# Re-planning a two-layer linear-attention kernel: DMA transposes given queue time, small matmuls cut into pieces between large ones, masks built first

## The chip, the cores and the metric

The kernel runs on one core of a Trainium2 chip. The metric is the device time of one launch in microseconds (us), and a quoted time is the median of several runs. For the matmul engine (TensorE, "PE" in the profile) the profile records a granted clock; in the recorded profiles it is 1.0 (full) or 0.5 (half) in every entry. "Granted clock" below is the mean of that over a run or a stretch. The other names in the profiles are PEld for PE's weight loads, DVE for VectorE, ACT for ScalarE, POOL for GpSimd, and SPq for the queue from which DMAs are issued; `L390` is line 390 of the kernel.

Runs of one kernel here differ by up to 2.7% (182.61 to 187.48 us for the kernel before, within one series), and a run that is over 1.5% above the fastest of the same kernel is marked "slow". Ratios below use fast runs alone.

## The reference, cut to what matters

```python
x = A_x                                              # 2048 x 512
x = x + attention(layernorm(x), wqkv, wo)            # layer 1
x = x + moe(layernorm(x), w_r, w_gate, w_up, w_down)
x = x + attention(layernorm(x), wqkv, wo)            # layer 2, the same weights
x = x + moe(layernorm(x), w_r, w_gate, w_up, w_down)

def attention(x, wqkv, wo):                          # 32 heads of 16, no softmax
    q, k, v = ...x @ wqkv...
    phi = lambda t: where(t > 0, t + 1, exp(t)) + 1e-6
    pq, pk = phi(q), phi(k)
    kv = einsum("bhsd,bhse->bhde", pk, v)            # sum over all 2048 rows
    z = einsum("bhsd->bhd", pk)                      # key sums, over all rows
    return (pq @ kv) / (pq @ z + 1e-6) @ wo

def moe(x, ...):                                     # two rows of 2048 are chosen
    r = x @ w_r                                      # router logits
    idx = argsort(-r)[:2]                            # the top two rows
    y = (silu(x[idx] @ w_gate) * (x[idx] @ w_up)) @ w_down
    return x + scatter(sigmoid(r[idx]) * y)
```

Every attention layer needs sums over all rows before its first output, and every MoE layer needs the logits of all rows before it can choose two.

## The kernel before

The rows are handled as 16 tiles of 128. For each tile the kernel makes `xn` (the normed tile), `xnT` (its transpose, by a DMA), and `K` (`xnT` times `wk`, then phi, giving `pk`). `G` accumulates `xn`ᵀ`pk` over the tiles. `Q` is one of 16 query products, `den` turns a quarter of the queries into queries divided by the denominator, and `O` is one of 16 outputs. Between the layers and after the last a top-2 search runs ("key search" below), and a small correction for the two chosen rows is put into `G` at the end of layer 2.

All instructions are first collected as a plan. The program's order is then chosen by a simple list scheduler, which works with assumed durations. So a line of the source moves many instructions, and a changed assumption does too. In the code below, `mm`, `g` and `tp` are pools of tiles in PSUM, the memory that the products of this kernel are written to.

```python
# the scheduler: the op that can start earliest goes next; ties go by priority
asked = t
if o.port:
    t = max(t, port_at["POOL" if e == "DVE" else "DVE"])
c = (t, asked, o.prio)
if best is None or c < best[0]:
    best = (c, o)
# ... cut ...
BUFS = {"mm": 3, "g": 4, "tp": 1, "e": 4, "em": 4, ...}   # mm, g, tp are PSUM

def trans(t):                      # assumed to hold the queue for 0.06 us
    def f():
        nc.sync.dma_start_transpose(out=xnT[:, :, t*P:(t+1)*P], in_=xn[:, t, :])
    op("SP", 0.06, f, r=[("xn", t)], w=[("xnT", t)])

def z_sum(layer, corr=None):       # key sums: one block of 64 one-column matmuls
    zc = ps("tp", [P, NC, 1])
    def f():
        for c in range(NC):
            for t in range(NT):
                T_.matmul(zc()[:, c, :], lhsT=pk[:, t, c*P:(c+1)*P], rhs=ones_b[:],
                          start=(t == 0), stop=(t == NT - 1 and corr is None))
            # ... cut: one correction matmul per c in layer 2 ...
    pe(1.7, f, r=[("pk", t) for t in range(NT)] + ..., w=[zc])

def r0_all():                      # logits: one block of 64 one-column matmuls
    # ... cut ...
    pe(1.7, f, r=[("xnT", t) for t in range(NT)] + ["wr"], w=[p])

def gate_up(p):                    # one block of 88 two-column matmuls
    # ... cut ...
    pe(2.35, f, r=["xs", ("wgu", 0), ("wgu", 1)], w=[p])

def den(layer, j):                 # two PSUM buffers, both from the single tp
    p, ..., sp, rd = ps("tp", [P, P]), ..., ps("tp", [P, NC, P]), ...

def consts():                      # masks, held back to 27 us
    pool(3.6, consts_gp, w=["masks0", "masks"], port=True).avail = 27.0
    pool(1.3, consts_gp2, w=["pid", "rid"], port=True).avail = 32.0
# ... cut ...
QA, QT = 11, 6        # limit of the Q products between the first layer's K and G
# ... cut ...
QB = 14               # Q products emitted before the first output
K2LAG = 6             # outputs before the second layer's first K
```

## Time and profile before

The time is 184.1 us (four runs, 183.7 to 184.4). It passes through seven stages. The table gives their ends and lengths in two profiles: the recorded one, and that of a variant of this kernel (`e2_before_masks_first` below, same time within 0.5%) which fell in a fast run.

| stage | recorded profile (slow run): end, length | fast profile: end, length |
|---|---|---|
| layer 1, up to its first output O | 66.70, 66.70 | 64.07, 64.07 |
| outputs O of layer 1 | 83.87, 17.17 | 81.64, 17.57 |
| transposes and K of layer 2, up to the key search | 96.49, 12.62 | 94.77, 13.13 |
| MoE of layer 1 beside K and G of layer 2, up to the last correction product | 130.71, 34.22 | 128.49, 33.72 |
| up to the first output of layer 2 | 142.57, 11.86 | 140.35, 11.86 |
| outputs of layer 2, up to the last key search | 169.53, 26.96 | 167.36, 27.01 |
| tail: last MoE and stores | 184.74, 15.21 | 182.34, 14.98 |

The page of the recorded profile: the first two lines give span and busy times. The three rows of digits cut the span in 40 slices of 4.6 us, each digit being a busy share in tenths; for PEclk it is the granted clock in tenths. (The record of the clock begins with the first full stretch, here at 7.24 us, so the row shows 9 before it too.)

```profile
span 184.7 us, 4083 instructions
PE 158.7 (86%) x1501; PEld 82.5 (45%) x1521; DVE 137.4 (74%) x469; ACT 98.1 (53%) x240; POOL 25.5 (14%) x55
PE   7989985999999879995949999999999999952580
DVE  0699986197878899998758857595349999996711
PEclk9999998799999999999987999999969999996555
```

PE is busy nearly everywhere, so it is the first suspect. But the row of digits has gaps (the 5 and 4 in the middle), and in the dips of PEclk the large products take twice their time (128x512 matmuls start 427 ns apart in each of the three dips before the tail, 216 ns apart at full clock). "Large" means at least 128 columns, "small" one or two, from here on. The same for the stages from the second on, with busy us of PE, PEld, DVE, ACT and POOL (and instructions), granted clock, DMA share and GB/s:

```profile
66.70:83.90 17.20, 16.42 (x151) 8.43 (x153) 16.75 (x70) 13.93 (x45) 1.51 (x2) 1.00 0.05 12
83.90:96.50 12.60, 8.20 (x36) 3.34 (x36) 9.13 (x42) 7.80 (x24) 2.37 (x3) 0.98 0.45 101
96.50:130.70 34.20, 33.79 (x283) 16.69 (x286) 24.24 (x85) 13.06 (x26) 1.60 (x4) 0.96 0.09 21
130.70:142.60 11.90, 11.58 (x160) 7.26 (x162) 7.30 (x16) 5.39 (x11) 0.00 (x0) 0.86 0.01 1
142.60:169.50 26.90, 21.53 (x205) 10.96 (x208) 26.40 (x98) 19.99 (x57) 4.76 (x7) 0.97 0.06 21
169.50:184.70 15.20, 7.51 (x206) 6.71 (x206) 4.81 (x21) 2.28 (x6) 5.83 (x8) 0.50 0.31 106
```

Read each line for the engine with the least idle time. The output stages are bound by VectorE (DVE: 16.75 of 17.20, 26.40 of 26.90), the third and fourth lines by PE (33.79 of 34.20, 11.58 of 11.90), and the second line, the transposes, by neither: there PE is busy 8.2 of 12.6 us. The waits of the whole kernel say why (engine and line, what it waited for, total us, times, longest; the second of these lines is the hole near 31 us, in layer 1):

```profile
PE mm L390 <- DMA xnT<-xn: 5.8, 5, 2.5
PE mm L390 <- DVE pqT L370: 2.0, 1, 2.0
```

The timeline of the DMA queue and of PE shows it in place (start, length, engine, line, operation, count, and in brackets the idle time before and what ended it):

```profile
81.23 21.95 SPq L354 DMA_TRANSPOSE xnT<-xn  x16
...
30.97 1.76 PE L390 MATMUL mm<-wk,xnT 128*128 128x512 bf16 x4 [2.01 <-DVE pqT L370]
...
65.06 0.38 PE L540 MATMUL tp<-rb,E 128*128 128x128 bf16 x4 [0.95 <-ACT rd L542]
66.13 0.41 PE L524 MATMUL tp<-pqT,Z 128*32 128x128 bf16 x16 [0.69 <-ACT rd L542]
...
83.60 1.04 PE L390 MATMUL mm<-wk,xnT 128*128 128x512 bf16 x4 [0.65 <-DMA xnT<-xn]
...
87.51 1.90 PE L390 MATMUL mm<-wk,xnT 128*128 128x512 bf16 x7 [1.57 <-DMA xnT<-xn]
...
95.38 1.32 PE L390 MATMUL mm<-wk,xnT 128*128 128x512 bf16 x4 [2.52 <-DMA xnT<-xn]
...
130.64 0.55 PE L438 MATMUL tp<-ones_b,pk 128*128 128x1 bf16 x16
...
133.23 1.18 PE L426 MATMUL mm<-xnT,wq 128*128 128x512 bf16 x3 [0.16 <-issue]
```

The second layer's 16 transposes start only at 81.2 us, when the outputs are nearly done, and PE waits for them (0.65, 1.57, 2.52 us, and 0.26 us in a line not shown: 5.0 us in all). The lines at 65.06 and 66.13 are the `den` of the single `tp` buffer: the second product waits until ScalarE has copied the first out (`rd`). From 130.64 to 133.07 PE works on nothing but one-column matmuls, the second layer's key sums.

Before the tail the trace has three stretches at half clock, from 31.14, 95.99 and 133.54 us, and each is 3.413 us long. The stretches at full clock before and between them and after the last are 7, 18, 10 and 9 times that (23.89, 61.44, 34.13 and 30.72 us).

### The profile page before, as it was taken

The page shows a single profiled execution, that of the slowest core. Times are in us where ns is not written, and L with a number is a line of the kernel's source. Part 1 is how long each engine was busy: PE and PEld are TensorE (multiplying, and loading weights), DVE is VectorE, ACT ScalarE, POOL GpSimd, SP SyncE. Part 2 cuts the span into 40 slices and gives each one's busy share as a digit, 9 for nine tenths or more (in the row PEclk, how much of TensorE's full clock was granted, in tenths as well). Part 3 has the DMA queues.
Part 4 walks back from the last instruction along what each step waited for, and adds up shares of the span by engine and source line. Part 5 has one row for each costly group of instructions (what it writes and reads, how often), then busy time and mean ns, then how long its engine had stood idle before and what let it go on. Part 6 is the DMA issues. An engine that isn't in the chain of part 4 may idle for free. (4 is left out here: it accounts for less than half of the span.)

```text
span 184.7 us, 4083 instructions
## 1 busy us (share of the span) xinstructions
PE 158.7 (86%) x1501; PEld 82.5 (45%) x1521; DVE 137.4 (74%) x469; ACT 98.1 (53%) x240; POOL 25.5 (14%) x55
## 2 busy tenths in 40 slices
PE   7989985999999879995949999999999999952580
PEld 2444342354467345541424475434654454532570
DVE  0699986197878899998758857595349999996711
ACT  2278854254454748798736125341237685888000
POOL 1111148000000000034101000000000000066900
PEclk9999998799999999999987999999969999996555
DMA  5995665999600000013443200000000000003450
GB/s 182 334 321 119 96 85 133 282 348 429 265 0 4 0 4 0 5 28 87 111 91 83 59 5 4 0 0 0 4 0 0 4 0 4 2 0 114 173 175 2
DMA packets 23589, 16.40 MB, mean 89 GB/s; under 512 B 17936, under 2 KB 21776, under 8 KB 23184
## 3 DMA queue, kind: packets, MB, share of 16 engines
q1 hardware_dynamic: 23272, 15.61, 29.7%
q10 hardware_dynamic: 296, 0.53, 0.8%
q8 instruction: 12, 0.20, 0.5%
q14 instruction: 9, 0.07, 0.1%
HBM read 9.83 MB, written 2.10 MB: 65 GB/s over the span
## 5 line engine op out<-in xcount | busy, mean ns | idle before, releaser
L359 ACT ACTIVATE e<-mm 128x512 bf16<-128x512 f32 x58 | 34.4, 595 | 46.1 <-PE mm L426 24.2
L390 PE MATMUL mm<-wk,xnT 128*128 128x512 bf16 x100 | 27.3, 404 | 8.1 <-DMA xnT<-xn 5.8
L426 PE MATMUL mm<-xnT,wq 128*128 128x512 bf16 x120 | 32.4, 389 | 0.6 <-issue 0.3
L414 PE MATMUL g<-pk,xn 128*128 128x512 bf16 x126 | 32.3, 387 | 0.3 <-issue 0.2
L558 PE MATMUL g<-KW,pqT 128*128 128x512 bf16 x122 | 29.1, 379 | 0.5 <-issue 0.3
L363 DVE TENSOR_SCALAR em<-e 128x512 bf16<-128x512 bf16 x58 | 16.5, 290 | 13.1 <-ACT e L359 12.9
L568 ACT ACTIVATE sq<-x 128x512 bf16<-128x512 bf16 x32 | 20.0, 625 | 5.1 <-DVE mv L578 2.2
L370 DVE SCALAR_TENSOR_TENSOR pqT<-mm,em 128x512 bf16<-128x512 f32 x32 | 21.7, 686 | 0.5
L390 PEld LDWEIGHTS <-xnT 128*128 128x128 bf16 x104 | 9.8, 102 | 21.6 <-DMA xnT<-xn 10.8
L414 PEld LDWEIGHTS <-xn 128*128 128x128 bf16 x128 | 12.4, 101 | 14.9 <-issue 1.3
L370 DVE SCALAR_TENSOR_TENSOR pk<-mm,em 128x512 bf16<-128x512 f32 x26 | 17.8, 685 | 0.4
L426 PEld LDWEIGHTS <-wq 128*128 128x128 bf16 x128 | 11.7, 100 | 13.3 <-issue 2.4
L558 PEld LDWEIGHTS <-pqT 128*128 128x128 bf16 x128 | 11.7, 97 | 12.5 <-DVE pqT L547 0.2
L1176 POOL TENSOR_SCALAR pk<-x,opr,nb 128x512 bf16<-128x512 bf16 x14 | 10.6, 769 | 47.7 <-DVE nb L1166 47.7
L313 DVE BATCH_NORM_STATS2 st<-x 128x6 f32<-128x512 bf16 x16 | 10.6, 679 | 4.9 <-DMA x<-in_A_x_dram 4.9
L564 DVE SCALAR_TENSOR_TENSOR x<-x,opr,g 128x512 bf16<-128x512 bf16 x16 | 11.4, 739 | 0.0
L347 POOL TENSOR_SCALAR xn<-x,s,nb 128x512 bf16<-128x512 bf16 x5 | 3.9, 785 | 52.2 <-PE g L558 48.3
L564 DVE SCALAR_TENSOR_TENSOR x<-x,g 128x512 bf16<-128x512 bf16 x16 | 10.7, 679 | 0.4 <-PE g L558 0.3
L547 DVE TENSOR_TENSOR pqT<-pqT,rd 128x1024 bf16<-128x1024 bf16 x16 | 10.4, 683 | 0.1
L347 POOL TENSOR_SCALAR xn<-x,rho,nb 128x512 bf16<-128x512 bf16 x6 | 4.6, 768 | 21.4 <-DVE nb L335 18.8
L401 PE MATMUL mm<-wk,xt 128*128 128x512 bf16 x24 | 6.3, 394 | 0.8 <-ACT rl L378 0.8
L864 PE MATMUL tp<-identf,s 128*128 128x128 f32 x8 | 2.3, 438 | 5.1 <-DVE s L860 5.1
(226 smaller groups left out, 212.0 us busy)
## 6 DMA issues: line engine op xcount, KB each, us to landing
wgu<-in_B_wgu_dram SPq DMA_DIRECT2D x2, 1408.0 KB, 10.0
out_dram<-pk SPq DMA_DIRECT2D x4, 512.0 KB, 3.2
wd<-in_B_wd_dram SPq DMA_DIRECT2D x1, 1408.0 KB, 12.9
x<-in_A_x_dram SPq DMA_DIRECT2D x2, 512.0 KB, 5.5
xt<-in_A_xt_dram SPq DMA_DIRECT2D x3, 256.0 KB, 4.5
x<-in_A_x_dram SPq DMA_DIRECT2D x3, 256.0 KB, 4.4
wk<-in_A_wk_dram ACTq DMA_DIRECT2D x2, 256.0 KB, 4.0
wq<-in_A_wq_dram SPq DMA_DIRECT2D x1, 512.0 KB, 6.6
```

The source lines that it names most:

```text
L313: dve(0.61, lambda: V.bn_stats(out=st()[:], in_=x[:, t, :]), r=[("x", t)], w=[st]).early = 4.0
L359: act(0.5, lambda: A.activation(out=e()[:], in_=p()[:], func=ACT.Exp), r=[p], w=[e], **k)
L363: dve(0.2, lambda: V.tensor_scalar(out=em()[:], in0=e()[:], scalar1=1.0, scalar2=TINY, op0=ALU.min, op1=ALU.add), r=[e], w=[em], port=True ...
L370: dve(0.6, lambda: V.scalar_tensor_tensor(out=out_ap, in0=p()[:], scalar=0.0, in1=em()[:], op0=ALU.max, op1=ALU.add), r=[p, em], w=[key], **k)
L390: T_.matmul(p()[:], lhsT=xnT[:, c, t * P : (t + 1) * P], rhs=wk[:, c, :], start=(c == 0), stop=(c == NC - 1))
L414: T_.matmul(Gs[c]()[:], lhsT=xn[:, t, c * P : (c + 1) * P], rhs=pk[:, t, :], start=(t == 0), stop=last and t == NT - 1,)
L426: T_.matmul(p()[:], lhsT=wq[:, i, c, :], rhs=xnT[:, i, j * D : (j + 1) * D], start=(i == 0), stop=(i == NC - 1))
L547: dve(0.6, lambda q=q: V.tensor_tensor(out=q, in0=q, in1=rd()[:].to_broadcast([P, 2, D]), op=ALU.mult), r=[rd], w=[("pq", j, c), ("pq", j, ...
L558: T_.matmul(p()[:], lhsT=pqT[:, j, c, tt * P : (tt + 1) * P], rhs=KWs[layer][:, c, :], start=(c == 0), stop=(c == NC - 1),)
L564: dve(0.64, lambda: V.scalar_tensor_tensor(out=x[:, t, :], in0=x[:, t, :], scalar=1.0 if i == 1 else opr[:, 0, t : t + 1], in1=p()[:], op0 ...
L568: act(0.6, lambda: A.activation(out=sq()[:], in_=x[:, t, :], func=ACT.Square, scale=float(D) ** -0.5, accum_out=sums[:, i, 1, t : t + 1],) ...
L1176: op(kind, 0.33 if kind == "DVE" else 0.76, lambda: e.tensor_scalar(out=xo[:, t, :], in0=x[:, t, :], scalar1=s_, scalar2=b_, op0=ALU.mult, ...
```

## The change

Its intent is to let the scheduler see what it had hidden from it, and to leave PE no stretch that is idle or full of small matmuls. No large product is added or removed. The parts:

1. A transpose holds the queue for 1.3 us in the plan, not 0.06. Other DMAs get plan times too.
2. Key sums and logits become groups of four matmuls, gate/up of layer 1 groups of twelve, and a rule in the scheduler avoids running small groups while large products filled less than half of the last 2.6 us (both figures are settings of the change).
3. The masks are built at the start, not held back to 27 us.
4. Counts: at most 8 instead of 11 Q products in layer 1's K stage, 10 instead of 14 before the first output, the second layer's K one output earlier.
5. The second buffer of `den` comes from `mm` (three buffers) instead of `tp` (one).

```diff
@@ the scheduler @@
-                    c = (t, asked, o.prio)
+                    c = (t, asked, o.prio + (8.0 if e == "PE" and o.st is not None and self.active(t) < 0.5 else 0.0))
+    def active(self, t, span=2.6):
+        return sum(min(d, max(0.0, s + d - t + span)) for s, d in self.mm[-40:] if s + d > t - span) / span
@@ trans @@
-        op("SP", 0.06, f, r=[("xn", t)], w=[("xnT", t)], **k)
+        op("SP", 1.3, f, r=[("xn", t)], w=[("xnT", t)], lat=1.35, **k)
@@ key sums @@
-    def z_sum(layer, corr=None):            # a block of 64
+    def z_piece(layer, zt, t, after=()):    # four matmuls, after each G
+        def f():
+            for c in range(NC):
+                T_.matmul(
+                    zt()[:, c : c + 1], lhsT=pk[:, t, c * P : (c + 1) * P], rhs=ones_b[:],
+                    start=first and c == 0, stop=layer == 0 and t == NT - 1, skip_group_check=True,
+                )
+        pl.lazy = 6.0
+        pe(0.11, f, r=[("pk", t), zt] + ..., w=[("z", layer, t)] + ...).st = 0.01
@@ logits: the same, r0_piece(t) @@
@@ den @@
-        p, ld, rb, sp, rd = ps("tp", [P, P]), ..., ps("tp", [P, NC, P]), ...
+        p, ld, rb, sp, rd = ps("tp", [P, P]), ..., ps("mm", [P, NC, P]), ...
@@ consts @@
-        pool(3.6, consts_gp, w=["masks0", "masks"], port=True).avail = 27.0
-        pool(1.3, consts_gp2, w=["pid", "rid"], port=True).avail = 32.0
+        pool(3.6, consts_gp, w=["masks0", "masks"])
+        pool(1.3, consts_gp2, w=["pid", "rid"])
@@ driver @@
-    QA, QT = 11, 6
+    QA, QT = 8, 6
-    QB = 14
+    QB = max(10, QA + 2)
-    K2LAG = 6
+    K2LAG = 5
-    gate_up(gu)
+    gate_up(gu, 3)
@@ cut: order of tiles as a list, names, two mask buffers to mm @@
```

## The prediction

> **What bounds the kernel now.** By the windows by stage: up to 66.7 us PE, with holes. From 66.7 to 84.0 (first attention output) DVE: 16.86 busy of 17.30. From 84.0 to 97.0 the DMA queue: PE is busy 8.60 of 13.0, the queue's timeline shows twelve transposes back to back from 81.2 to 96.8, one per 1.30 us, and the waits show 5 us of PE holes behind "DMA xnT<-xn". From 97.0 to 130.6 PE (33.2 of 33.6). From 142.6 to 169.4 DVE (26.4 of 26.8), then a serial tail of 15 us.

> The granted clock falls to half for about 3.4 us three times: at 31-36 after a 2.0 us PE hole (POOL built masks and slowed the DVE: an em took 0.51 instead of 0.29, an nb 0.63 instead of 0.15), at 95-99 after the transpose hole, at 133-137 after the second key sum (68 one-column matmuls, 2.4 us). Each costs about 1.7 us of PE time. [...]

> **What the change does** (from the instruction order of both):
> - No matmul work goes away. Two key sums (1.74 and 2.43 us) and the logits (1.74) become groups of 4, about 0.11 us each (27 ns per matmul in the trace); PE work stays within 1 us.
> - Masks precede the norms on POOL: about 5 us, in its idle time before 8.6 us. The hole at 29-31 and its slow clock go: -3.5.
> - Seven instead of nine Q products precede the last first-layer G; two run in the output stage. First output about 5 us earlier (61-62), but that stage carries about 2.3 us more DVE work, so it ends only about 3 us earlier (81).
> - The first second-layer norms come after 9 outputs, not 13; transposes start near 74 instead of 81.2 and the last ends near 97-98 instead of 103. PE holes there shrink from 5 to 1-2 us; the half clock mostly goes. The PE-bound stage ends near 124-125 instead of 130.6.
> - After it, no block of key sums and no half clock: 8.5 us from the last G to the first output instead of 12. But the DVE work from there to the final top-k, about 34 us, is unchanged and binds; its idle time falls from 4.8 to perhaps 2-3. Top-k near 161-162 instead of 169.3.
> - The tail (gate/up in one piece there) is unchanged: 15.2.

> **Time.** 184.3 - 3 (first layer, after the DVE's extra work) - 3.5 (transposes) - 1.5 (DVE fed earlier) would be 176.3; I give back 0.7 for new waits (three `mm` buffers now also serve denominators, masks and the second key sum): 177.0, range 173.0 to 181.0. Chances: faster 0.84, same 0.14, slower 0.02.

> **What would show it.** Granted clock full from 18 us to the final top-k, mean near 0.95; no PE hole over 1 us at 25-35; first transposes of layer two near 74, with gaps between groups of four rather than PE holes; key-sum pieces of 0.1 us; last-stage DVE still about 98% busy; tail 15 us.

> **What would make it wrong.** PE stalling on `mm` buffers; the small groups costing much more than 0.11 us between products; the second layer's transposes still setting the pace; POOL's early masks delaying DVE statistics (the DVE is 10.0 of 10.0 busy at 10-20 us).

The sum: 184.3 − 3 − 3.5 − 1.5 + 0.7 = 177.0.

## The result, and the profile after

The changed kernel takes 176.24 us (four runs, 174.9 to 177.6) against 184.09 us before. The ratio is 0.9551, with a 95% interval of 0.9492 to 0.9611. A ratio here is the mean time of one kernel's fast runs over that of the other's fast runs of the same rounds, so it is not quite the ratio of the medians. The change is faster by 4.5%, and the total lies 0.8 us below the predicted one.

The page of the changed kernel, the same lines as before (this run is a slow one):

```profile
span 175.4 us, 4072 instructions
PE 155.2 (88%) x1500; PEld 80.7 (46%) x1521; DVE 137.5 (78%) x469; ACT 98.9 (56%) x240; POOL 25.7 (15%) x55
PE   7899989999999999998999999999999999922580
DVE  1569997786688899998999858268989999995501
PEclk9999999999999999999999999999999999995555
```

The gaps in the PE row are gone, and so are all dips of PEclk before the last slices. By stage:

```profile
62.00:82.20 20.20, 19.40 (x182) 9.79 (x183) 19.59 (x78) 15.86 (x49) 1.74 (x2) 1.00 0.18 28
82.20:90.50 8.30, 8.03 (x37) 3.59 (x37) 7.92 (x37) 7.48 (x21) 2.47 (x3) 1.00 0.28 63
90.50:125.00 34.50, 33.79 (x346) 17.85 (x349) 25.65 (x93) 13.84 (x29) 1.61 (x4) 1.00 0.18 33
125.00:131.90 6.90, 6.79 (x86) 3.64 (x87) 6.38 (x12) 5.11 (x11) 0.00 (x0) 1.00 0.00 0
131.90:160.80 28.90, 21.93 (x206) 10.96 (x207) 28.01 (x99) 19.68 (x56) 8.49 (x12) 0.94 0.11 38
160.80:175.50 14.70, 7.54 (x206) 6.71 (x206) 3.67 (x21) 2.65 (x7) 2.12 (x3) 0.50 0.21 74
```

Compare it line by line with the table of before. The transpose stage shrank from 12.6 to 8.3 us with PE's busy time nearly the same (8.20, 8.03): what went was waiting. The stage before the second layer's outputs shrank from 11.9 to 6.9 us, because PE's busy time fell from 11.58 to 6.79: the block of key sums (133.07 − 130.64 = 2.43 us) was done earlier, between large products, and no half-clock window is left in it (granted clock 0.86 before, 1.00 after); that is, by my estimate, about 2.4 + 1.7 (half of 3.41) of the 4.8 us. The rest, fewer Q products in the stage, is a matter of order. The 26.9 us output stage grew to 28.9 us (DVE 28.01 busy of 28.90). It holds no more Q products than before (19 of their matmuls on record in both). What differs is that POOL runs twelve output instructions in it instead of seven, the five others having come from the tail, and that DVE's small statistics take longer (four `s<-mv,nwr,rr` 1.40 instead of 0.85 us, four `mv<-mv,sums` 1.12 instead of 0.62). That one causes the other is not shown. The waits and the timelines:

```profile
PE mm L401 <- DMA xnT<-xn: 1.5, 2, 0.9
```

```profile
75.65 25.42 SPq L365 DMA_TRANSPOSE xnT<-xn  x16
...
34.00 0.24 PE L460 MATMUL tp<-ones_b,pk 128*128 128x1 bf16 x4
34.10 1.02 PE L401 MATMUL mm<-wk,xnT 128*128 128x512 bf16 x4
...
79.55 1.04 PE L401 MATMUL mm<-wk,xnT 128*128 128x512 bf16 x4 [0.60 <-DMA xnT<-xn]
...
81.29 3.06 PE L401 MATMUL mm<-wk,xnT 128*128 128x512 bf16 x12
84.43 2.75 PE L425 MATMUL g<-pk,xn 128*128 128x512 bf16 x12
```

The transposes start at 75.65 instead of 81.23, and the waits for them fall from 5.8 to 1.5 us in the whole kernel. In the second layer alone they fall from 5.0 to 0.60 us; the rest is a wait near 24 us in layer 1 (0.84 before, 0.87 after). A key-sum group delays the next large product by 0.10 us (34.00 to 34.10). From 81 on PE runs without a hole of note.

**Where the time went, in fast runs.** Two variants that change no time but fell in fast runs, with similar starts, make a cleaner pair than the recorded profiles: `e2_before_masks_first` (182.34 us) and `e1_masks_moved` (172.71 us), both described below. Their spans differ by 9.63 us, more than the 8 us of the medians, since the second is one of its kernel's faster runs.

| stage | before's stand-in | after's stand-in | gain |
|---|---|---|---|
| to the last G product of layer 1 | 48.60 | 47.33 | 1.27 |
| to the first output | 15.47 | 12.60 | 2.87 |
| outputs of layer 1 | 17.57 | 19.59 | −2.02 |
| transposes and K of layer 2 | 13.13 | 8.29 | 4.84 |
| MoE of layer 1, G of layer 2 | 33.72 | 34.45 | −0.73 |
| to the first output of layer 2 | 11.86 | 6.98 | 4.88 |
| outputs of layer 2 | 27.01 | 28.85 | −1.84 |
| tail | 14.98 | 14.62 | 0.36 |

Counting PE alone up to its last product before the final key search says the same in two terms. The sum of its holes over 0.15 us is 11.59 us in the first and 5.15 in the second, a gain of 6.44. The first spends 6.83 us at half clock, the second none; since large products take twice their time at half clock (427 against 216 ns above), that is worth up to 6.83 / 2 = 3.41 us. Together 9.85, and the last product ended 162.23 − 151.84 = 10.39 us earlier. So the gain is PE time recovered: about two thirds from holes, one third from the clock. This is bookkeeping of one engine's time and must come out near the total. It does not say which part of the change removed which hole, nor whether DVE would have allowed the gain without the rest.

### The profile page after: what moved, and what is told of

The parts are those of the page before. It is cut to its first block, busy times and chain, and to the rows that moved or that the text cites. A ratio compares the mean times of both kernels' runs of the same rounds, so it can differ in the third digit from the quotient of the medians.

```text
span 175.4 us, 4072 instructions
## 1 busy us (share of the span) xinstructions
PE 155.2 (88%) x1500; PEld 80.7 (46%) x1521; DVE 137.5 (78%) x469; ACT 98.9 (56%) x240; POOL 25.7 (15%) x55
## 5 line engine op out<-in xcount | busy, mean ns | idle before, releaser
L436 PE MATMUL mm<-xnT,wq 128*128 128x512 bf16 x120 | 31.7, 379 | 1.0 <-DVE pqT L381 0.6
L425 PE MATMUL g<-pk,xn 128*128 128x512 bf16 x123 | 31.3, 378 | 0.4
L582 PE MATMUL g<-KW,pqT 128*128 128x512 bf16 x124 | 29.7, 379 | 0.7 <-DVE pqT L570 0.4
L401 PE MATMUL mm<-wk,xnT 128*128 128x512 bf16 x101 | 25.4, 379 | 1.8 <-DMA xnT<-xn 1.5
L425 PEld LDWEIGHTS <-xn 128*128 128x128 bf16 x128 | 11.6, 98 | 12.2 <-issue 0.4
L1208 POOL TENSOR_SCALAR pk<-x,opr,nb 128x512 bf16<-128x512 bf16 x14 | 10.6, 774 | 39.3 <-DVE nb L1198 39.3
L324 DVE BATCH_NORM_STATS2 st<-x 128x6 f32<-128x512 bf16 x16 | 10.7, 682 | 5.1 <-DMA x<-in_A_x_dram 4.9
L588 DVE SCALAR_TENSOR_TENSOR x<-x,g 128x512 bf16<-128x512 bf16 x16 | 10.7, 679 | 0.5 <-PE g L582 0.5
L570 DVE TENSOR_TENSOR pqT<-pqT,rd 128x1024 bf16<-128x1024 bf16 x16 | 10.6, 686 | 0.1
L338 ACT ACTIVATE lnv<-mv,eps_t 128x2 f32<-128x2 f32 (+2 forms) x18 | 5.1, 292 | 7.8 <-DVE mv L325 5.1
L412 PE MATMUL mm<-wk,xt 128*128 128x512 bf16 x23 | 7.7, 467 | 0.1
```

The source lines that it names most:

```text
L324: dve(0.61, lambda: V.bn_stats(out=st()[:], in_=x[:, t, :]), r=[("x", t)], w=[st]).early = 4.0
L401: T_.matmul(p()[:], lhsT=xnT[:, c, t * P : (t + 1) * P], rhs=wk[:, c, :], start=(c == 0), stop=(c == NC - 1))
L425: T_.matmul(Gs[c]()[:], lhsT=xn[:, t, c * P : (c + 1) * P], rhs=pk[:, t, :], start=first, stop=last)
L436: T_.matmul(p()[:], lhsT=wq[:, i, c, :], rhs=xnT[:, i, j * D : (j + 1) * D], start=(i == 0), stop=(i == NC - 1))
L570: dve(0.6, lambda q=q: V.tensor_tensor(out=q, in0=q, in1=rd()[:].to_broadcast([P, 2, D]), op=ALU.mult), r=[rd], w=[("pq", j, c), ("pq", j, ...
L582: T_.matmul(p()[:], lhsT=pqT[:, j, c, tt * P : (tt + 1) * P], rhs=KWs[layer][:, c, :], start=(c == 0), stop=(c == NC - 1),)
```

## The experiments

Times are medians; ratios are to the kernel before, in rounds of the same chip. The changed kernel has 0.9551. Most edits that undo a part let the scheduler plan anew, so the order changes broadly with them. Four edits keep the changed kernel's order otherwise: `e1_masks_moved`, `e1_z1_block`, `e1_spin10` and `e2_z1_double`.

Three cautions. The medians count one slow run each of `e1_masks_moved`, `e1_z1_block` and `e2_z1_double` (fast runs alone: 175.37, 175.04 and 179.06); the ratios do not. The e1, e2 and e3 runs ran on three chips, on which the kernel before took 184.57, 184.25 and 184.29. And in three profiles of the changed order with no other loss (`e1_masks_moved`, the control and the recorded one) the span goes with the moment of the first full clock: this is at 5.39, 9.43 and 10.58 us, and the spans are 172.71, 174.42 and 175.44 us. The moment is known for profiled runs only, so a difference of 1 to 2 us between two kernels is weak evidence unless their starts are alike.

| run | us | ratio, 95% interval |
|---|---|---|
| e1_control (changed kernel again) | 175.66 | 0.9543, 0.9473 to 0.9613 |
| e1_masks_moved | 175.96 | 0.9552, 0.9479 to 0.9625 |
| e1_z1_block | 175.68 | 0.9525, 0.9461 to 0.9589 |
| e1_spin10 | 174.43 | 0.9480, 0.9439 to 0.9522 |
| e2_before_masks_first | 184.38 | 1.0042, 0.9959 to 1.0124 |
| e2_counts_of_before | 175.08 | 0.9514, 0.9454 to 0.9574 |
| e2_queue_free | 176.77 | 0.9617, 0.9551 to 0.9682 |
| e2_z1_double | 179.18 | 0.9772, 0.9673 to 0.9870 |
| e3_before_den_mm | 184.13 | 1.0009, 0.9945 to 1.0072 |
| e3_after_den_tp | 177.45 | 0.9660, 0.9604 to 0.9716 |
| e3_after_blocks | 180.13 | 0.9782, 0.9740 to 0.9824 |
| e3_counts_spin_warm | 174.29 | 0.9466, 0.9432 to 0.9500 |

### e1_control: the changed kernel, unedited

> The changed kernel itself, unedited, as the yardstick for the three runs beside it. All theories: 0.950 to 0.961 of the time before (its first measurement gave 0.9551), full clock from about 10 us to the last key search.

It took 175.66 us (174.5 to 177.0) and repeats the result. Its own spread, 1.4%, is the measure for what follows.

### e1_masks_moved and e2_before_masks_first: do the masks matter?

In the finished order of the changed kernel, the masks are put back behind the fifth norm on GpSimd (POOL):

```diff
-        for o in pl.order():
+        seq = pl.order()
+        masks = next(o for o in seq if getattr(o, "tag", "") == "masks")
+        norms = [o for o in seq if o.eng == "POOL" and o.dur == 0.76]
+        seq.remove(masks)
+        seq.insert(seq.index(norms[4]) + 1, masks)
+        for o in seq:
```

> The 3.6 us block of masks goes back behind the fifth POOL norm (near 27 us, where it was before); the order on every other engine is that of the changed kernel. Theory of the prediction (the masks slowed the DVE, which made the 2.0 us hole and the half clock): a PE hole of 1.5 to 2.5 us near 30 us comes back, a half-clock stretch of 3.4 us follows it, and the run is 2 to 4 us slower than the control. Rival (the hole of before was PE running ahead of the transposes: the tile's transpose landed at 30.92 us, 0.02 us before the buffer came free; in the changed kernel PE arrives there later because its start is 2 us later): no hole over 0.5 us, full clock, within 0.7 us of the control, although single DVE instructions beside the masks are longer.

The time was 175.96 us, and neither a hole near 30 us nor a slow clock came back. The other way round, the kernel before gets its masks first:

```diff
-        pool(3.6, consts_gp, w=["masks0", "masks"], port=True).avail = 27.0
-        pool(1.3, consts_gp2, w=["pid", "rid"], port=True).avail = 32.0
+        pool(3.6, consts_gp, w=["masks0", "masks"])
+        pool(1.3, consts_gp2, w=["pid", "rid"])
```

> The kernel before with one part of the change alone: the masks are built first on POOL (its planner then also places the small products that depend on them elsewhere). Theory of the prediction (masks cause the hole near 30 us and the half clock after it): both go, the first attention output comes about 3 us earlier, the time falls by 2 to 3.5 us (0.981 to 0.990 of before). Rival (the hole is PE waiting for the transpose that lands near 31 us, the masks are only beside it): a hole of 1 us or more stays within 28 to 33 us, a half-clock stretch follows in the profile, and the time is within 1 us of before.

Nothing again: 184.38 us. From its page, the granted clock, and from its PE timeline, the hole:

```profile
PEclk9999999999999999999978999999879999995555
```

```profile
30.14 1.04 PE L390 MATMUL mm<-wk,xnT 128*128 128x512 bf16 x4 [1.60 <-DMA xnT<-xn]
```

The hole near 30 us stays (1.60 us) with no mask work beside it, and it ends with a transpose. The masks were not its cause. (The rival's half-clock stretch after it did not come either.) The PEclk row has the dips of a fast run of before: two (91 to 100 us and 128 to 137 us), not the three of the recorded profile. The missing one is that of 31 to 36 us. The mean granted clock of 29 runs of the kernel before bears this out. By estimate, time at half clock is 2 × (1 − clock) × span (24.1 us in this profile: two windows of 3.41 us and 17.2 us, mostly the tail). With 17.1 us put down to the tail, the 18 runs at a clock of 0.933 to 0.937 have two more windows of 3.41 us, three at 0.942 have one, and only runs marked slow, at 0.929 and below, have three or four. So a third window, in the recorded profile the one at 31 us, belongs to slow runs of the kernel before, and no gain over its fast runs can come from it. Masks first do not prevent it: two of the four runs of `e2_before_masks_first` have a clock of 0.924, which means a third window somewhere, though they count as fast.

### e1_z1_block: the second layer's key sums as one block, in the changed order

```diff
+        for tag in ['z1']:
+            mine = [o for o in seq if getattr(o, "tag", "") == tag]
+            at = seq.index(mine[-1])
+            seq = [o for o in seq[:at] if o not in mine] + mine + seq[at + 1 :]
```

> The sixteen key-sum pieces of the second layer are run as one block of 64 one-column matmuls where the last piece stood (near 121 us); nothing else moves. Theory (a block of tiny matmuls makes the clock fall): the block takes 1.7 to 2.0 us, a half-clock stretch of 3.4 us appears within 5 us after it, and the last key search is 1 to 2.5 us later. Rival (only the place of the pieces counts, PE work is the same and the DVE binds from there on): full clock, the last key search within 0.5 us of the control, because PE has given the DVE work in advance.

The time was 175.68 us: a block of 64 one-column matmuls alone costs nothing in this place. By windows around the block (same columns as the stage tables):

```profile
119.30:122.70 3.40, 3.35 (x76) 2.35 (x74) 2.23 (x6) 1.18 (x2) 0.00 (x0) 1.00 0.02 5
122.70:126.10 3.40, 3.40 (x31) 1.20 (x29) 3.25 (x9) 2.49 (x6) 0.00 (x0) 1.00 0.00 0
```

The window after the block still ran at full clock. About 52% of the first window went to large products (1.78 of 3.41 us, each counted from its start to the next instruction's). Whether a window with hardly any large products would do it was my next question, and the doubled block its test.

### e2_z1_double: the same block, its matmuls run twice

The block's first piece runs all 64 matmuls once more (a second pass starts the accumulation anew; the run's output is correct).

```diff
+            if layer == 1 and first:
+                for u in range(NT):
+                    for c in range(NC):
+                        T_.matmul(zt()[:, c : c + 1], lhsT=pk[:, u, c * P : (c + 1) * P], rhs=ones_b[:], ...)
```

> As the block run, but the block of the second layer's key sum runs twice over (128 one-column matmuls; the second pass restarts the sums, so the result stays right): about 3.5 us of tiny matmuls in one piece, 1.73 us more PE work than the changed kernel. Theory [...]: a half-clock stretch of 3.4 us begins within 4 us of the block's end; first output of the second layer 2.5 to 4 us later. Rival ([...] the half clock of before at 133.5 us had another cause): full clock to the end, first output 1.7 us later.

What had been measured is the single block: 1.74 us of small matmuls beside 1.78 us of large products, and 1.00 in the next window.

The time was 179.18 us; by fast runs alone it is 179.06 against 175.04 us for the single block, 4.0 us more.

```profile
117.10:120.50 3.40, 3.40 (x124) 3.16 (x123) 2.16 (x5) 0.80 (x2) 0.00 (x0) 1.00 0.02 5
120.50:123.90 3.40, 3.40 (x27) 1.36 (x25) 0.75 (x4) 0.60 (x1) 0.00 (x0) 0.50 0.00 0
```

PE was busy for the whole of the first window, and the clock still fell to 0.50 in the next. So the clock fell without idle time of PE: the first window held 3.02 us of one-column matmuls and 0.38 us of large products. The last correction product ended at 125.55 instead of 122.26 us (`e1_masks_moved`), and the final key search came at 161.37 instead of 158.09. These 3.3 us are 1.73 us of added matmuls and about 1.7 us (half of 3.41) of slow clock, and they reach the end in full: DVE's slack in the last stage takes up none of them.

### e3_after_blocks: key sums, logits and gate/up of the changed kernel as blocks again

`z_piece` and `r0_piece` emit one operation of 64 matmuls for the last tile, and gate/up is one piece:

```diff
-    gate_up(gu, 3)
+    gate_up(gu, 2 * NF)
-        pe(0.11, f, r=[("pk", t), zt] + ...).st = 0.01
+        pe(1.76, f, r=[("pk", u) for u in range(NT)] + [zt], w=[("z", layer, u) for u in range(NT)] + ["zf%d" % layer])
```

(The scheduler also got a check that enough buffers are free for all that one operation asks. Planned again with this check alone, the changed kernel keeps its order; that was done off the chip.)

> The changed kernel with key sums, logits and gate/up in whole blocks again, planned again. Theory (small pieces give a good part of the gain, through the clock and through gaps that they fill): at least one half-clock stretch in the profile, time 2 to 5 us above 175.7. Rival (the block run beside the control was as fast as the control, so a block of 1.75 us costs nothing in itself): full clock, within 1 us of 175.7.

The time was 180.13 us, 4.5 us more than the control, and in all four runs the mean clock was 0.928 to 0.930. The windows and the PE timeline show where:

```profile
48.26:51.67 3.41, 3.41 (x134) 3.32 (x131) 1.14 (x2) 0.46 (x1) 0.00 (x0) 1.00 1.00 423
51.67:55.08 3.41, 3.19 (x36) 2.31 (x35) 2.17 (x12) 0.60 (x1) 0.00 (x0) 0.50 0.18 68
102.87:106.28 3.41, 3.40 (x94) 2.77 (x94) 2.21 (x7) 1.19 (x2) 0.00 (x0) 1.00 0.01 2
106.28:109.69 3.41, 3.29 (x17) 1.37 (x17) 2.00 (x7) 0.79 (x3) 0.00 (x0) 0.50 0.01 2
```

```profile
48.08 1.74 PE L462 MATMUL tp<-ones_b,pk 128*128 128x1 bf16 x64
...
103.93 2.34 PE L959 MATMUL tp<-xs,wgu 128*128 128x2 bf16 x88
```

Key sums, logits and some more one-column matmuls in a row filled a window; the 88 two-column matmuls of gate/up filled 2.34 us of another, in which 1.06 us (31%) went to large products. PE had no idle time in either, and after each came a window at half clock. PE's account agrees: 3.4 us of slow clock and 1.6 us more holes than in the control make 5.0, and its last product before the final key search ended 4.7 us later. So cutting the small matmuls is the largest of the parts that were undone. Two reservations: the order moved too (the stretch from the first output to the first key search grew from 28.1 to 34.5 us, with 15 instead of 3 Q matmuls in it, and the next stage shrank), and this run does not tell what the block of key sums and logits costs from what gate/up costs. In the recorded profile of before, the same block of 88 (at 107.65 us) fell so that 42% of its window went to large products, and the next window had full clock.

### e2_queue_free: the changed kernel, its DMAs costless in the plan again

```diff
-        op("SP", 1.3, f, r=[("xn", t)], w=[("xnT", t)], lat=1.35, **k)
+        op("SP", 0.06, f, r=[("xn", t)], w=[("xnT", t)], **k)
```

(and the two plan times of the loads and stores likewise.)

> The changed kernel planned again with the queue costs of before (a transpose, a load and a store take 0.06 us of the queue in the plan). Theory (the queue's time in the plan matters): PE waits of 2 us or more in total for transposes between 76 and 100 us, a half-clock stretch there, time 2 to 5 us above 175.7. Rival (counts and pieces made the gain): PE waits for transposes stay under 1.5 us in total, full clock, time within 1 us of 175.7.

The time was 176.77 us, 1.1 us more than the control, which their intervals do not resolve. Set beside `e1_masks_moved`, whose profile has a like start (full clock at 5.39 us, here 4.72), its span is 2.0 us longer (174.75 against 172.71). PE's holes before the final key search summed to 6.66 us against about 5.1 us; 4.1 us of them lie in the first 25 us, against 3.1 in the control. At the second layer's transposes PE waited only about 0.9 us, so the long wait there did not come back without the plan's queue time. Neither side of the expectation held in full: the waits and the clock are the rival's, the time lies just outside its 1 us.

### e2_counts_of_before: the changed kernel with the counts of before

```diff
-    QA, QT = 8, 6
+    QA, QT = 11, 6
-    QB = max(10, QA + 2)
+    QB = max(14, QA + 2)
-    K2LAG = 5
+    K2LAG = 6
```

> The changed kernel with the three counts of before: 11 Q products before the key sums, 14 before the output stage, second-layer keys 6 outputs behind instead of 8, 10 and 5; the planner reorders accordingly. Theory (the counts give the earlier output stage and the earlier transposes): first output 2 to 4 us later, first second-layer transpose 2 us later or more, time 1.5 to 4 us above the changed kernel's 175.7. Rival (the queue's time in the plan gives it, counts are secondary): time within 1 us of 175.7.

The time was 175.08 us (174.96 to 175.18): no loss that shows. The landmarks did move the way that the theory said (first output 61.55, first transpose 76.28 us, against 59.93 and 73.54 in `e1_masks_moved`, with a like start), but the outputs of layer 1 then took 17.1 instead of 19.6 us. The span is 0.6 us longer than there (173.30 against 172.71), so what the counts gave is about 0.6 us by one profile of each, which is not resolved.

### e3_before_den_mm and e3_after_den_tp: the denominator's buffer

```diff
-        p, ld, rb, sp, rd = ps("tp", [P, P]), ..., ps("tp", [P, NC, P]), ...
+        p, ld, rb, sp, rd = ps("tp", [P, P]), ..., ps("mm", [P, NC, P]), ...
```

This in the kernel before, and the reverse in the changed one.

> The kernel before with one unannounced part of the change alone: the spread of the reciprocal denominators writes an `mm` buffer instead of the single `tp` buffer that the denominators themselves need (plus a planner check that four free buffers are there when four are asked for). Theory (the single buffer chained the denominators, which shows as PE holes of 0.95 and 0.69 us before the first output): the holes go, first output 1.5 to 3 us earlier, time 1 to 3 us lower (0.984 to 0.995). Rival (other engines take it up again, the queue's transposes still set the pace to 97 us): first output earlier, but the last second-layer transpose and the time within 0.7 us of before.

> The changed kernel with that one part undone (denominator spread back in the single `tp` buffer), planned again. Theory (that buffer matters): PE holes near 55 to 65 us and first output 1.5 to 3 us later, time 1.5 to 4 us above 175.7. Rival: within 1 us of 175.7.

In the kernel before, the two holes at 65 and 66 us went (0.95 and 0.69), and the first output came at 62.51 instead of 64.07 us. Yet the time was 184.13 us, the same. The mean clock was 0.916 to 0.923 in all four runs: three half-clock windows where the usual run has two (in the profile from 84.72, 105.20 and 129.09 us). What the buffer gave, the clock took back: PE's holes are 1.9 us smaller than in `e2_before_masks_first`, its half-clock time is 3.41 us longer, which costs 1.7. In the changed kernel, taking the buffer away cost 1.8 us (177.45), and PE's holes rose from about 5.1 to 8.8 us. The intervals of this run and of the control just touch, and the span is 2.0 us longer than that of `e1_masks_moved`, with a like start. But the expected place was wrong: the first output came at 60.19 us, no later than in `e1_masks_moved` (59.93), and the added holes lie from 65 to 100 us, most of them where PE waits for `pk` from DVE. Why the buffer costs time there is not shown.

### e1_spin10: why runs of the changed kernel spread by 1.4%

The kernel starts with eight dummy matmuls of no use to the result (in the control they fill PE from 1.28 to 4.87 us). Two more were added:

```diff
-            for _ in range(n):
+            for _ in range(n + 2):
```

> Ten warm-up matmuls instead of eight, the order otherwise the same: fills the 0.83 us hole at 4.9 us in which PE waits for the first transposed input. Theory A ([...] the full clock came at 10.6 us instead of 7.2): full clock near 7.2 us, first layer's first K products about 1.5 us earlier. Then, if PE paces the first 30 us, the run is 1 to 2 us faster than the control; if the transposes pace it (theory of the rival above), a PE hole appears near 24 to 31 us instead and the time stays within 0.7 us.

(The two moments are those of the recorded profiles, 10.58 and 7.24 us.)

The time was 174.43 us, 1.2 us below the control, and its six runs lie within 0.8 us (the control's within 2.5). The start of PE, first in the control and then here:

```profile
5.65 1.01 PE L757 MATMUL tp<-xt,nmean 128*128 128x256 bf16 x4 [0.77 <-DMA xt<-in_A_xt_dram]
6.46 3.36 PE L412 MATMUL mm<-wk,xt 128*128 128x512 bf16 x8
```

```profile
5.79 0.60 PE L757 MATMUL tp<-xt,nmean 128*128 128x256 bf16 x4
6.22 1.89 PE L412 MATMUL mm<-wk,xt 128*128 128x512 bf16 x8
```

The dummies ended before the first load landed, and left a hole of 0.77 us. With it filled, the first eight K products took 1.89 instead of 3.36 us; the clock was full from 5.81 us on, in the control from 9.43. In the profiles of the changed kernel and its variants with eight dummies, the full clock began anywhere between 4.5 and 10.7 us. That this phase is what made its runs differ fits the three spans given above and the narrow spread here in the one kernel whose hole is filled; the phase of its other runs is not on record.

### e3_counts_spin_warm: the best parts together, and a warm tail

The counts of before, ten dummies, and 44 dummy matmuls while PE waits for the final key search:

```diff
+            for _ in range(44 if i == 1 else 0):
+                T_.matmul(p()[:], lhsT=warm[:, 0:P], rhs=warm[:, 0 : 2 * P], start=True, stop=True)
```

> An attempt to beat both: the changed kernel with the counts of before (175.1), ten warm-up matmuls instead of eight (174.4 alone), and 44 matmuls of no use between the last product and the final key search, which keep the clock up in the serial tail. Theory: the gains add where they touch different stretches: 173.0 to 174.2, of which the warm tail gives 0.6 (the key search takes 0.6 us instead of 1.2). Rival (the counts' 175.1 was only a lucky phase of the start): 174.0 to 174.6.

The time was 174.29 us, just outside the 173.0 to 174.2 that the theory gave and inside the rival's range, by which the counts had only had a lucky start. The tail did get shorter: final key search to end 14.49 us against 15.20 with the counts alone, the search's four products 0.71 against 1.22 us. The mean clock was 0.963 to 0.973 in its six runs, against 0.947 and 0.948 with the counts alone. The total is still no better than ten dummies alone. It and `e1_spin10` are the fastest kernels, about 0.8% below the changed kernel; the intervals overlap the control's.

Not tried on the chip: the kernel before with nothing but the queue time of transposes, for which the scheduler, run off the chip, finds no order (with the old latency beside the new queue time it does), and the kernel before with nothing but the small matmuls in pieces, which is the obvious counterpart of `e3_after_blocks`.

## Why the prediction was right or wrong

**The total was right, and most of its landmarks.** Predicted 177.0, measured 176.24. The first output was expected at 61 to 62 us (62.04), the end of the layer's outputs near 81 (82.2), the end of the PE-bound stage at 124 to 125 (124.9), and the final key search at 161 to 162 (160.8). There was no hole over 1 us at 25 to 35, the mean clock was 0.948 (near 0.95 expected), the pieces cost 0.10 us, and the last stage's DVE was 97% busy. Part of this agreement is luck: baseline and result are both slow runs, with full clock from 7.24 and 10.58 us, and in the fast control the same landmarks lie about 1 us earlier (61.34, 81.2, 123.9 and 159.8); and the terms of the sum erred in both directions, as shown below. The mechanism, holes and slow stretches of PE taken away and DVE fed earlier, is what the PE account of the fast pair shows (holes 11.59 to 5.15 us, half clock 6.83 to 0 us).

**"Masks precede the norms… The hole at 29-31 and its slow clock go: -3.5." This step failed.** Moving the masks back in the changed kernel costs nothing, and moving them first in the kernel before gains nothing and leaves a 1.60 us hole. I had read slowed DVE operations (`em` and `nb`, named by the tiles that they write) beside the mask work as the cause. Whether the mask work slows DVE at all is left open: `em` took 0.40 and 0.42 us beside it in `e1_masks_moved` (at 27.41 and 30.35 us), and the control has `em` of 0.41 and 0.46 us at 28.82 and 30.57 us, with no mask work near them; one `nb` took 0.22 us beside the masks, and 0.15 us in the control. In the kernel before, the K product at 30.97 was released by a transpose landing at 30.92 and a DVE result at 30.94, so a faster DVE alone could not have freed it. And its half-clock window belongs to slow runs. Why the hole is gone in the changed order stays open: no part that was undone brings it back.

**The number of half-clock stretches was one too many.** I counted three, at 1.7 us each, from a profile of a slow run. The usual fast run of before has two. I should have checked the profiled run's clock against the others before I costed from it. The total came out because other terms were larger than I had them.

**The Q counts were thought to bring the first output forward.** "Seven instead of nine Q products precede the last first-layer G" is eight instead of nine in the traces, and the run with the counts of before is about as fast. They move DVE work from one stage to another: in the stage table, 2.87 us before the first output and −2.02 us in the outputs.

**"First transposes near 74… the last ends near 97-98."** They started at 75.65, and the last was issued at 99.2 us and landed between 102 and 103. Between groups the queue idled. It did no harm, as by then PE had other work; the holes of the second layer fell further than predicted (5 to 1 or 2 us), from 5.0 to 0.60. The stage shrank by 4.3 us in the recorded profiles, where the sum had -3.5 for the transposes.

**Terms that were mis-sized.** The first layer was put at −3; the end of its outputs moved from 83.87 to 82.18, so −1.7 (−2.1 in the fast pair). The stage from last correction to first output was put at 8.5 us after the change and took 7.0. "DVE fed earlier" was put at −1.5: from the correction's end to the final key search it took 38.82 before and 35.89 after, so −2.9. DVE's idle time in it fell from 5.1 to 1.4 us, more than the 2 to 3 that I had left it. The tail lost 0.6 us, unforeseen. So one term was too large and three too small, and they nearly cancel. That the last outputs were done earlier, leaving POOL and DVE less to do there (5.83 to 2.12 and 4.81 to 3.67 us busy), fits this, but no run tests it.

**The denominator's buffer was not costed as a gain.** I named it only as a risk ("new waits"). Undone, it costs about 1.8 us, with intervals that just touch. Alone in the kernel before it gives nothing.

**No single part tried makes this gain.** In the kernel before, masks first gave 0 and the buffer gave 0, the latter because a half-clock window came back. Taken from the changed kernel, the small pieces cost 4.5 us, the buffer 1.8, the queue time 1 to 2 (unresolved), masks and counts nothing that shows. These do not add up to 8, and need not: each undone part was planned into a new order. Most of the holes' share of the gain is therefore not traced to a single part; of the parts tried alone, only the small pieces show a loss whose interval is clear of the control's.

## What to carry to other kernels

Before costing from a profile, check that its clock is that of the usual run, and count slow-clock stretches over many runs. Cut blocks of one- and two-column matmuls into groups between large products: a group of four delayed the next large product by 0.10 us, but in these fourteen profiles each of the 22 windows of 3.41 us that left less than 40% to large products was followed by one at half clock. A block of about 2 us did or did not make such a window by where it fell: the 88 matmuls of gate/up (2.34 us) left 42% to large products in the recorded profile of before, and the next window had full clock; in `e3_after_blocks` they left 31%, and the next had half clock. Undo each part of a planned change on its own, since a part that looks like the cause may give nothing, and a part that nobody announced may carry a good share.

## Further figures measured here

- Half clock followed a window whose longest gap on PE was 2.52 us (before, at 95 us), and one without any (`e2_z1_double`, PE busy 3.40 of 3.40 us).
- 64 one-column matmuls of `e3_after_blocks` took 1.68 us from their start to the next instruction's (48.08 to 49.76), 26 ns each. Those of `tp<-pqT,Z` (128*32 128x128 in the profile) start closer: in the recorded profile of after, 96 of 120 start 3 or 4 ns after the one before, the other 24 from 45 to 57 ns after it.
- Half clock hardly slowed the 88 two-column matmuls of gate/up: they took 2.34 us at full clock (before, at 107.65 us) and 2.49 us at half (at 175.40 us).
- A DMA transpose of a 128x512 bf16 tile, 131,072 bytes within SBUF, took 1.30 us of the queue when transposes followed each other (before, from 81.23 us), which is 101 GB/s.
